# A Mamba-2 scan followed by a SiLU layer: one more pair of units multiplied in seven products, with the plain second product of the first two units moved between

## The chip, the cores and the metric

The kernel runs on one NeuronCore of one Trainium2 chip. TensorE (PE in the profile) multiplies and writes to PSUM. VectorE (DVE), ScalarE (ACT) and GpSimd (POOL) work beside it, and SyncE (SP) issues most of the DMAs. Each engine takes its own instructions in program order, and waits on semaphores that the others raise. The metric is the device time of one execution in microseconds (us), and the number compared is the median of several runs. Before the change it is 359.44 us, the median of 3 runs from 358.6 to 359.83 us.

## The reference, cut to what matters

A state-space scan over 4 batches, 8 heads and 768 positions (head size 32, state size 16) gives a 3072 x 256 matrix, and a two-matrix layer with SiLU follows:

```
cum = cumsum(log(clip(a, 1e-6, 1)));  L = exp(cum_i - cum_j), causal, by chunk
y   = ((C B^T) * L) x  +  (C state) * exp(cum)          # then state is carried on
x   = y as (batch * seq, heads * head_dim)              # 3072 x 256
h   = x @ w_in                                          # 256 -> 2048
g   = h / (1 + exp(-h))                                 # SiLU
out = g @ w_out                                         # 2048 -> 256
```

The weights arrive as 64-bit floats. The kernel loads them as pairs of 32-bit words and rebuilds fp32 values on the chip.

## The kernel before, in words

The 3072 rows are cut into 12 units of 256 positions, three to a batch. A unit first goes through the scan, in pieces named after their functions: P (prefix product of the decays, lines 278 and 284), E (the decay triangle: clip at 315 and scan at 297), T and T2 (B and C transposed, `ce` at 359), B (`BT`, line 334) and C (`cw`, line 365), D and G (small products in PSUM tile `gy`, lines 383 and 398), S (states, line 424), M (mask times product, line 409), Y (the unit's output in PSUM, lines 452 and 461) and X (its copy to `XM`, line 470). Then comes the **first product** with `w_in`, SiLU, and the **second product** with `w_out`.

Either product can be done in two ways.

- *Plain.* `f_s1(g, j)` (line 481) does the first product of one unit: in each of eight steps j, two blocks of 128 columns with two products each, and one SiLU over both. `s2_list` (line 495) does the plain second product of units one after the other: 64 products of 128 x 128 by 256 for two units, summed in one PSUM bank (`o_ps`, a pool of one buffer), with two copies by ScalarE (line 500) and four stores when a unit is done.
- *In seven.* Two units are taken together as the two columns of a 2 x 2 block matrix, and multiplied with seven block products where the plain way takes eight (Winograd's form of Strassen's scheme). For that, sums and differences are made beforehand. Those of the weights are `SW` (first product, line 627) and `SO` (second product, line 526), made once. Those of the data are `XT` (first product, line 638) and `TN` with changes in place of `gT` (second product, `f_TS`, line 540), made for each pair.

`f_x1(G, j, ...)` is a step of the first product in seven for pair G. It uses three PSUM tiles, X, W and Y. The seven products are named W, 1, 5, 6, 7, 4 and 3, and a string in `ORDER`, one for each j, gives their order; each "s" in it is one product of a second product, drawn from the queue `S2` by `f_s2(1)`, to fill TensorE. Products 1, 6, 7 and 4 all go to X: 6 adds to what 1 left there, and must wait until ScalarE has copied X (`p1`); 7 adds again after the next copy (`u2`); 4 adds after VectorE has read X for an add (line 658). Product 5 and product 3 go to Y, and W has its own tile. Between these, a list of scan pieces for the next pair is worked off on VectorE and ScalarE (`scan_plan` and `other`).

Before the change, units 0 to 3 use the plain first product, and units 4 to 11 go in pairs G = 2 to 5. The second product is plain for units 0 and 1 and in seven for all later pairs. The order by hand at the end of the kernel is this:

1. a start in which the inputs come in, the first two scans run, weight pieces are rebuilt (`w_size` on ScalarE, `w_bits` on VectorE at lines 174 to 178 and GpSimd at line 182), and `busy(n)` gives TensorE products of zeros;
2. `steps`: the first product of units 0 and 1, mixed with weight pieces and the scan of unit 2;
3. eight steps of `f_s1(2, j)`, each with a piece of unit 3's scan and four plain second products;
4. eight steps of `f_s1(3, j)`, each with pieces of the scans of units 4 and 5 and four plain second products; `SO`, `XT` and the first sums of pair 1 are made here too;
5. pairs G = 2 to 5 with `f_x1`, filled with the second product of the pair before, and at the end the second product of pair 5.

Every engine's queue is in program order, so a piece that waits holds up all that stands behind it on its engine. `f_P01` (lines 270 and 273) makes the prefix products of units 0 and 1 together, in the start.

Of the kernel before, what the change touches and what calls it, by code (L numbers as in the profile page):

```python
# [21 lines left out]
def kernel(  # L22
# [22 lines left out]
    nc = tc.nc  # L45
# [169 lines left out]
    idle = early[:, 4].bitcast(BF16)  # L215
    nc.vector.memset(idle, 0.0)

    def busy(n, early=True):
        t = ps_o.tile([128, 512], FP32, name="o_ps") if early else ps_s.tile([128, 4, 512], FP32, name="gy")[:, 0]
        for i in range(n):  # L220
            nc.tensor.matmul(out=t, lhsT=idle[:, 0:128], rhs=idle, start=True, stop=True)

    nc.vector.memset(ach[0:A0], 0.0)

# [12 lines left out]
                                fill=1.0, base=-64 * c, channel_multiplier=1)  # L237
    tiny = const.tile([128, 1], FP32, name="tiny")
    nc.scalar.activation(tiny, idle[:, 0:1], AF.Silu)
    busy(5)  # L240
    f_A()
    ident = const.tile([128, 128], FP32, name="ident")
    nc.vector.memset(ident, 0.0)
# [23 lines left out]

    def f_P01():

        nc.vector.tensor_scalar(out=pz01.rearrange("p (c t) -> p c t", c=8)[:, :, 1:],  # L270
                                in0=pa01.rearrange("p (c t) -> p c t", c=8), scalar1=1.0, scalar2=1e-6,
                                op0=ALU.min, op1=ALU.max)
        nc.vector.tensor_tensor_scan(out=pfx01, data0=pz01, data1=one01, initial=0.0, op0=ALU.mult, op1=ALU.add)  # L273
        for u in range(2):
            PFX[u] = pfx01.rearrange("p (c t) -> p c t", c=8)[:, 4 * u:4 * u + 4]
# [212 lines left out]
    def s2_list(units):  # L488
        for g in units:
            b, t0 = at(g)  # L490
            r = out[b * S + t0:b * S + t0 + UT].rearrange("(k c i) m -> k i c m", k=2, c=2)
            o = ps_o.tile([128, 2, d_model], FP32, name="o_ps")
            for c in range(2):
                for f in range(NF):
                    nc.tensor.matmul(out=o[:, c], lhsT=GTS[g][:, f, 128 * c:128 * c + 128], rhs=w_out_sb[:, f, :],  # L495
                                     start=(f == 0), stop=(f == NF - 1), skip_group_check=True)
                    if f == NF - 1 and c == 1:
                        for e in range(2):
                            o_sb = ppool.tile([128, UT], FP32, name="ps")
                            nc.scalar.activation(o_sb, o[:, e], AF.Copy)  # L500
                            for k in range(2):
                                nc.sync.dma_start(out=r[k][:, e], in_=o_sb[64 * k:64 * k + 64])
                    yield
# [108 lines left out]


    wj = w_in_sb.rearrange("p k (j i f) -> p k i j f", i=2, f=128)
    SW, XT = [], []

    def spare(d, n):
        t = rawp.tile([128, 2, WF, 2], U32, name="raw").bitcast(FP32)
        return t.rearrange("p k f two -> p (k f two)").rearrange("p (a b) -> p a b", b=n) if d is None else t

    def f_SW(i):

        t = spare(None, 128)
        SW.append(t)
        a0, a1, op = ((wj[:, 0, 1], wj[:, 1, 1], ALU.add), (SW[0], wj[:, 0, 0], ALU.subtract),
                      (wj[:, 0, 0], wj[:, 0, 1], ALU.subtract), (wj[:, 1, 0], SW[min(i, 1)], ALU.subtract))[i]
        nc.gpsimd.tensor_tensor(out=t, in0=a0, in1=a1, op=op)

    def xm2(u):
        return XM[u].rearrange("p (w c) t -> p w (c t)", w=2)  # L630

    def f_XT(G, i):

        if len(XT) < 2 and i == 0:
            XT.append(spare(None, UT))
        t, b0, b1 = XT[G % 2], xm2(2 * G), xm2(2 * G + 1)
        a0, a1 = ((b1[:, 0], b0[:, 0]), (b1[:, 1], t[:, 0]), (b1[:, 1], b1[:, 0]), (b0[:, 1], t[:, 1]))[i]
        nc.gpsimd.tensor_tensor(out=t[:, i], in0=a0, in1=a1, op=ALU.subtract)
# [2 lines left out]

    ORDER = ("W15s6sss7sss43", "W1s56ss7sss43s", "W1ss56ss7ss43s", "W1sss56ss7ss43",
             "W1ss6ss57sss43", "W1sss6ss57ss43", "W1s56sss7ss43s", "W1s56sss7sss43")

    def f_x1(G, j, dve, act):
        u0, u1 = 2 * G, 2 * G + 1
        if j == 0:
            for u in (u0, u1):
                GTS[u] = gpool.tile([128, NF, UT], FP32, name="gT")
        g0, g1, t = GTS[u0], GTS[u1], XT[G % 2]  # L650
        b0, b1 = xm2(u0), xm2(u1)
        X, W, Y = (ps_h.tile([128, 512], FP32, name="hp")[:, 0:UT] for _ in range(3))

        def mm(o, w, x_, start=True):
            nc.tensor.matmul(out=o, lhsT=w, rhs=x_, start=start, stop=True, skip_group_check=True)  # L655

        def add(o, p, q):
            nc.vector.tensor_tensor(out=o, in0=p, in1=q, op=ALU.add)  # L658

        def silu(o, i):  # L660
            nc.scalar.activation(o, i, AF.Silu)  # L661

        def other(todo, n):
            for _ in range(min(n, len(todo))):
                todo.pop(0)()

        def copy(name, i):
            o = sc.tile([128, UT], FP32, name=name)
            nc.scalar.activation(o, i, AF.Copy)  # L669
            return o  # L670

        done, first = "", 3 if j in (1, 4) else 2
        for what in ORDER[j]:
            done += what
            if what == "s":
                f_s2(1)
            elif what == "W":
                mm(W, wj[:, 1, 0, j], b0[:, 1])
            elif what == "1":
                mm(X, wj[:, 0, 0, j], b0[:, 0])  # L680
                p1 = copy("p1", X)
                add(g0[:, 2 * j], W, p1)
                other(dve, 2 if j in (2, 5) else 0)
            elif what == "5":
                mm(Y, SW[0][:, j], t[:, 0])
                p5 = copy("p5", Y)
            elif what == "6":
                mm(X, SW[1][:, j], t[:, 1], False)
                u2 = copy("u2", X)
                silu(g0[:, 2 * j], g0[:, 2 * j])  # L690
                other(dve, first)
            elif what == "7":
                mm(X, SW[2][:, j], t[:, 2], False)
                add(g1[:, 2 * j + 1], X, p5)
                silu(g1[:, 2 * j + 1], g1[:, 2 * j + 1])
            elif what == "4":
                mm(X, wj[:, 1, 1, j], t[:, 3], False)
                silu(g0[:, 2 * j + 1], X)
                other(dve, 2)
            elif what == "3":  # L700
                mm(Y, SW[3][:, j], b1[:, 1], False)
                add(g1[:, 2 * j], Y, u2)
                silu(g1[:, 2 * j], g1[:, 2 * j])
            if what in "56" and "5" in done and "6" in done:
                other(act, 9)
        other(dve, 9)
        assert not dve and not act
        if j == 7:
            XM.pop(u0)
            XM.pop(u1)  # L710
# [33 lines left out]
    def scan_plan(G):  # L744
        plan = [([], [], []) for _ in range(8)]
        for i in range(2):
            u, j = 2 * G + i, 3 * i
            E0 = [partial(f_E0, u, q, 2) for q in range(2)]
            E1 = [partial(f_E1, u, q, 4) for q in range(4)]
            plan[j][0].extend([partial(f_P0, u), partial(f_P1, u), E0[0], E0[1], E1[0], E1[1]])  # L750
            plan[j][1].extend([partial(f_T2, u, 0), partial(f_T2, u, 1)])
            plan[j + 1][0].extend([E1[2], E1[3], partial(f_B, u), partial(f_C, u)])
            plan[j + 1][2].append(partial(f_G, u))
            plan[j + 2][0].extend([partial(f_S, u, 0, 2), partial(f_S, u, 2, 4), partial(f_M, u, 0),
                                   partial(f_M, u, 1)])
# [12 lines left out]
    f_Ab(0, 0)  # L768
    f_Ab(0, 1)
    f_G0(0)  # L770
    busy(4)
    f_Ek(0, 0)
    f_Ek(0, 1)
    f_B(0)
# [8 lines left out]
    w_bits(0, 2)  # L783
    f_Ab(1, 0)
    w_size(1)
    busy(4)
    f_Y(0)
    f_Ab(1, 1)
    f_X(0)
# [36 lines left out]
            else:  # L826
                scan_piece(2, 0, step)

    for g, j, todo in steps:
        f_s1(g, j)  # L830
        w_steps(todo)
    load_unit(3)
    late = ("b13 s14", "b14 s15", "b15")
    S2.append(s2_list((0, 1)))
    for j in range(8):
        f_s1(2, j)
        scan_piece(3, j, ("", "", "T", "E", "BS", "G", "S", "Y"))
        f_s2(4)
        if j < len(late):
            w_steps(late[j])  # L840
        if j in (2, 5):
            load_unit(4 + j // 3)

    def sums(P, qs):

# [1 line left out]
            f_TS(P, 0, q, nc.gpsimd)  # L847
            f_TS(P, 2, q, nc.gpsimd)

    for j in range(8):  # L850
        f_s1(3, j)
        scan_piece(4, j, ("TE", "BS", "G", "Y", "", "", "", ""))
        scan_piece(5, j, ("", "", "T", "E", "BS", "G", "Y", ""))
        scan_piece(6, j, ("",) * 7 + ("t",))
        f_s2(4)
        if j in (2, 5):
            load_unit(6 + j // 3)
        if j in (1, 4, 6, 7):
            f_SO(len(SO))
        if j == 7:  # L860
            for i in range(4):
                f_XT(2, i)
        if j == 5:
            sums(1, (0, 1))
    for G in range(2, NU // 2):
        S2.append(s2_pair(G - 1))
        more = G + 1 < NU // 2
        plan = scan_plan(G + 1) if more else [([], [], []) for _ in range(8)]
        for j, (dve, act, pe) in enumerate(plan):
# [4 lines left out]
            for what in waiting:  # L874
                what()

            if j == 1:
                sums(G - 1, (2, 3) if G == 2 else (3,))
            if j == 1 or j == 4:
                for q in range(4):  # L880
                    f_TS(G - 1, (1, 3)[j // 4], q, nc.gpsimd)
            if j == 6 and more:
                for i in range(4):
                    f_XT(G + 1, i)
# [45 lines left out]
```

## Time and profile before

| what | value |
|---|---|
| median of 3 runs | 359.44 us |
| span of the profiled execution | 356.3 us |
| TensorE busy | 344.3 us (97%), 3276 records |
| VectorE busy | 183.2 us (51%) |
| ScalarE busy | 160.7 us (45%) |
| GpSimd busy | 181.9 us (51%) |
| share of PE in the chain that ended last | 91% |
| mean granted TensorE clock | 0.996 |
| DMA, mean over the span | 74 GB/s |

A line of the timeline gives start and length in us, the engine, the line of the kernel, the operation, tiles written and read, shape, how many instructions were merged, and in brackets the idle time before and what ended it. An fp32 product of 128 x 128 by 256 appears as two TensorE records. A record's busy time overlaps that of the next one, so the spacing of starts, and not the mean length, is what a product takes out of TensorE's time. Slices of busy time say which engine is full in which stage: an average over the whole span hides that VectorE is 93% busy from 27.65 to 55.31 us (25.75 of 27.66 us), and 46% busy from 116.97 to 170.82 us.

### The profile page before, as it was taken

To read this page: it belongs to the slowest core of one execution; us is meant where nothing else is said; L and a number is where in the kernel's file an instruction comes from. 1 tells how busy PE (TensorE), PEld (TensorE's weight loads), DVE (VectorE), ACT (ScalarE), POOL (GpSimd) and SP (SyncE) were. 2 spreads that over 40 slices of the span, in tenths; PEclk is the share of its full clock that TensorE was granted. 3 is DMA by queue.
4 is the path that set the end of the run, shared out by engine and by line. 5 is a ranking of instruction groups with operands and counts; after the bars stand their busy time and mean duration, and the time that the engine had idled before them with its cause. 6 is when DMAs were issued, how large, how long until landed. Compare 5 with 4: busy or idle time off the path is not lost.

```text
span 356.3 us, 8309 instructions
## 1 busy us (share of the span) xinstructions
PE 344.3 (97%) x3276; PEld 289.0 (81%) x3277; DVE 183.2 (51%) x389; ACT 160.7 (45%) x390; POOL 181.9 (51%) x246
## 2 busy tenths in 40 slices
PE   7879999999999999999999999999999999999994
PEld 2457888888888888888888888888888888888883
DVE  7978999554447444643454633455632221214722
ACT  2649575223222545545544545544545454453100
POOL 4434345524059076498274398264398930596100
PEclk9999999999999999999999999999999999999998
DMA  6898966871455270161026253110001010001203
GB/s 118 211 338 139 328 192 113 139 115 50 99 109 76 63 110 7 46 110 29 15 53 108 44 99 42 16 18 2 15 2 18 15 17 0 15 2 20 40 2 45
DMA packets 110059, 26.53 MB, mean 74 GB/s; under 512 B 98884, under 2 KB 105796, under 8 KB 110020
## 3 DMA queue, kind: packets, MB, share of 16 engines
q1 hardware_dynamic: 107044, 25.67, 35.5%
q10 hardware_dynamic: 2976, 0.33, 0.6%
q8 instruction: 26, 0.43, 0.5%
q14 instruction: 13, 0.11, 0.1%
HBM read 22.83 MB, written 3.15 MB: 73 GB/s over the span
## 4 chain that ended last, share of the span: by engine, by line
PE 91%; DVE 4%; DMA 2%; issue 1%; POOL 0%; SPq 0%; ACT 0%; ACTq 0%; DVEq 0%
PE o_ps L572 30%; PE hp L655 28%; PE hp L481 15%; PE o_ps L495 8%; PE hp L572 3%; PE gy L461 3%; PE gy L452 2%; PE gy L398 2%; DVE E L297 1%; PE gy L383 1%; DVE wv L178 1%; DMA tbc<-in_C_dram 1%; DMA tbc<-in_B_dram 1%; DMA out_dram<-ot 0%; DVE gT L273 0%
## 5 line engine op out<-in xcount | busy, mean ns | idle before, releaser
L658 DVE TENSOR_TENSOR gT<-hp,p 128x256 f32<-128x256 f32 x64 | 26.9, 420 | 84.6 <-ACT p L669 47.5
L481 PE MATMUL hp<-XM,w_in_sb 128*128 128x256 f32 x256 | 59.4, 381 | 1.9 <-POOL w_in_sb L182 1.1
L661 ACT ACTIVATE gT<-gT 128x256 f32<-128x256 f32 x96 | 39.7, 413 | 42.8 <-DVE gT L658 42.8
L334 POOL TENSOR_TENSOR BT<-bn,E 128x256 f32<-128x256 f32 x12 | 9.0, 751 | 94.5 <-PE hp L655 29.6
L572 PE MATMUL o_ps<-gT,w_out_sb 128*128 128x256 f32 x224 | 56.5, 379 | 0.0
L481 PEld LDWEIGHTS hp<-XM,w_in_sb 128*128 128x128 f32 x256 | 48.0, 190 | 9.7 <-POOL w_in_sb L182 2.4
L655 PE MATMUL hp<-raw 128*128 128x256 f32 x192 | 52.7, 380 | 0.0
L540 POOL TENSOR_TENSOR gT<-gT 128x256 f32<-128x256 f32 x72 | 51.3, 745 | 0.0
L572 PEld LDWEIGHTS o_ps<-gT,w_out_sb 128*128 128x128 f32 x224 | 42.4, 190 | 5.9
L655 PEld LDWEIGHTS hp<-raw 128*128 128x128 f32 x192 | 36.2, 190 | 5.4 <-POOL ps L543 0.6
L483 ACT ACTIVATE gT<-hp 128x512 f32<-128x512 f32 x32 | 19.1, 596 | 40.1 <-PE hp L481 40.1
L669 ACT ACTIVATE p<-hp 128x256 f32<-128x256 f32 x64 | 24.6, 384 | 27.5 <-PE hp L655 25.7
L658 DVE TENSOR_TENSOR gT<-hp,u 128x256 f32<-128x256 f32 x32 | 13.6, 424 | 40.8 <-PE hp L655 40.8
L655 PE MATMUL hp<-XM,w_in_sb 128*128 128x256 f32 x128 | 34.1, 389 | 0.0
L543 POOL TENSOR_TENSOR ps<-ps 128x256 f32<-128x256 f32 x28 | 20.4, 729 | 26.0 <-ACT ps L579 12.7
L495 PE MATMUL o_ps<-w_out_sb,gT 128*128 128x256 f32 x128 | 30.9, 384 | 0.0
L540 POOL TENSOR_TENSOR TN<-gT 128x256 f32<-128x256 f32 x40 | 28.8, 745 | 0.0
L495 PEld LDWEIGHTS o_ps<-w_out_sb,gT 128*128 128x128 f32 x128 | 23.8, 190 | 3.8 <-issue 0.5
L655 PEld LDWEIGHTS hp<-XM,w_in_sb 128*128 128x128 f32 x128 | 23.3, 190 | 4.3 <-issue 1.0
L297 DVE TENSOR_TENSOR_SCAN E<-ab,diag 128x256 f32<-128x256 f32 (+1 forms) x32 | 24.5, 804 | 3.7 <-PE gy L461 3.4
L540 POOL TENSOR_TENSOR gT<-gT,TN 128x256 f32<-128x256 f32 x32 | 22.2, 743 | 0.0
L579 ACT ACTIVATE ps<-o_ps 128x256 f32<-128x256 f32 x31 | 11.9, 384 | 18.5 <-PE o_ps L572 18.1
(121 smaller groups left out, 543.0 us busy)
## 6 DMA issues: line engine op xcount, KB each, us to landing
ab<-in_a_dram SPq DMA_DIRECT2D x40, 128.0 KB, 3.7
raw<-in_moe_w_in_dram SPq DMA_DIRECT2D x8, 512.0 KB, 8.1
raw<-in_moe_w_out_dram SPq DMA_DIRECT2D x8, 512.0 KB, 6.5
xt<-in_x_dram SPq DMA_DIRECT2D x24, 128.0 KB, 4.1
out_dram<-ot SPq DMA_DIRECT2D x76, 32.0 KB, 1.7
bn<-in_B_dram SPq DMA_DIRECT2D x22, 64.0 KB, 5.1
tbc<-in_C_dram SPq DMA_DIRECT2D x40, 32.0 KB, 2.1
pa<-in_a_dram SPq DMA_DIRECT2D x10, 128.0 KB
```

What stands on the lines that cost most here:

```text
L297: nc.vector.tensor_tensor_scan(out=E[u].rearrange("p k h t -> p (k h t)")[:, Q * g0:Q * (g0 + n)], data0=t.rearrange("p g t -> p (g t)"), ...
L481: nc.tensor.matmul(out=hp[:, i], lhsT=w_in_sb[:, kc, f * 128:(f + 1) * 128], rhs=xm[:, kc], start=(kc == 0), stop=(kc == KC - 1))
L483: nc.scalar.activation(GTS[g][:, 2 * j:2 * j + 2], hp, AF.Silu)
L495: nc.tensor.matmul(out=o[:, c], lhsT=GTS[g][:, f, 128 * c:128 * c + 128], rhs=w_out_sb[:, f, :], start=(f == 0), stop=(f == NF - 1), skip_ ...
L540: engine.tensor_tensor(out=o[:, j], in0=a0[:, j], in1=a1[:, j], op=ALU.subtract)
L543: engine.tensor_tensor(out=o, in0=p, in1=q, op=ALU.add)
L572: nc.tensor.matmul(out=o, lhsT=w(j), rhs=g()[:, j], start=(j == 0), stop=(j == NF // 2 - 1))
L579: nc.scalar.activation(pn, on, AF.Copy)
L655: nc.tensor.matmul(out=o, lhsT=w, rhs=x_, start=start, stop=True, skip_group_check=True)
L658: nc.vector.tensor_tensor(out=o, in0=p, in1=q, op=ALU.add)
L661: nc.scalar.activation(o, i, AF.Silu)
L669: nc.scalar.activation(o, i, AF.Copy)
```

## The change

Units 2 and 3 (pair G = 1) also go through `f_x1`. For this, unit 3's scan and `SW` must be complete before the pair begins, so a gap opens in the first products between units 0 and 1 and the pair. It is filled with 40 of the 64 plain second products of units 0 and 1; the other 24 go between the products of the pair, by new strings `ORDER1`. The loop over pairs starts at 1 in place of 2. Around it:

- `SW` is made on VectorE in place of GpSimd;
- the clip in `f_P01` (line 270) is made on GpSimd in place of VectorE;
- `s2_list` runs over f outside and over the two column blocks inside, so that its first products need only the first weight pieces;
- the loads of units 3, 4 and 5 are issued at other points, and the sums of pair 1 and the pieces of `SO` move into the steps of G = 1;
- one piece of the E scan of units 4 and 5 moves one step ahead;
- the products of zeros become 64 x 64 x 64 in place of 128 x 128 x 512, and 40, 24 and 32 in place of 5, 4 and 4.

```diff
     def busy(n):
-            nc.tensor.matmul(out=t, lhsT=idle[:, 0:128], rhs=idle, start=True, stop=True)
+            nc.tensor.matmul(out=t[:64, :64], lhsT=idle[:, 0:64], rhs=idle[:, 64:128], start=True, stop=True)
...
-    busy(5)
+    busy(40)
...
-        nc.vector.tensor_scalar(out=pz01.rearrange("p (c t) -> p c t", c=8)[:, :, 1:],
+        nc.gpsimd.tensor_scalar(out=pz01.rearrange("p (c t) -> p c t", c=8)[:, :, 1:],
...
-            for c in range(2):
-                for f in range(NF):
+            for f in range(NF):
+                for c in range(2):
...
-        nc.gpsimd.tensor_tensor(out=t, in0=a0, in1=a1, op=op)
+        nc.vector.tensor_tensor(out=t, in0=a0, in1=a1, op=op)
...
+    ORDER1 = ("W1ss56s7s43",) + ("W15s6s7s43",) * 7
...
-        for what in ORDER[j]:
+        for what in (ORDER1 if G == 1 else ORDER)[j]:
...
+            n = 3 if G == 2 else 2
+            plan[j][0].extend([partial(f_P0, u), partial(f_P1, u), E0[0], E0[1]] + E1[:n])
...
-    busy(4)
+    busy(24)
...
-    busy(4)
+    busy(32)
...
-    for j in range(8):
-        f_s1(2, j)
-        scan_piece(3, j, ("", "", "T", "E", "BS", "G", "S", "Y"))
-        f_s2(4)
...
+    for n, what in ((8, "b13 s14"), (6, "b14 s15"), (6, "T b15"), (6, "E D C"), (6, "S G"), (8, "S S S Y")):
+        f_s2(n)
...
+    load_unit(5)
+    for i in range(4):
+        f_XT(1, i)
+    for i in range(2):
+        f_T(4, i)
...
-    for j in range(8):
-        f_s1(3, j)
-        scan_piece(4, j, ("TE", "BS", "G", "Y", "", "", "", ""))
-        scan_piece(5, j, ("", "", "T", "E", "BS", "G", "Y", ""))
-        f_s2(4)
...
-    for G in range(2, NU // 2):
-        S2.append(s2_pair(G - 1))
+    for G in range(1, NU // 2):
+        if G > 1:
+            S2.append(s2_pair(G - 1))
...
+            if j in (1, 5, 6, 7) and G == 1:
+                f_SO(len(SO))
```

More of the change, by code (lines that the diff above doesn't have):

```diff
@@ L216, with busy @@
     nc.vector.memset(idle, 0.0)
-    def busy(n, early=True):
-        t = ps_o.tile([128, 512], FP32, name="o_ps") if early else ps_s.tile([128, 4, 512], FP32, name="gy")[:, 0]
+    def busy(n):
+        t = ps_o.tile([128, 512], FP32, name="o_ps")
         for i in range(n):
-            nc.tensor.matmul(out=t, lhsT=idle[:, 0:128], rhs=idle, start=True, stop=True)
+            nc.tensor.matmul(out=t[:64, :64], lhsT=idle[:, 0:64], rhs=idle[:, 64:128], start=True, stop=True)
     nc.vector.memset(ach[0:A0], 0.0)
@@ L492, in s2_list @@
             o = ps_o.tile([128, 2, d_model], FP32, name="o_ps")
-            for c in range(2):
-                for f in range(NF):
+            for f in range(NF):
+                for c in range(2):
                     nc.tensor.matmul(out=o[:, c], lhsT=GTS[g][:, f, 128 * c:128 * c + 128], rhs=w_out_sb[:, f, :],
-                                     start=(f == 0), stop=(f == NF - 1), skip_group_check=True)
+                                     start=(f == 0 and c == 0), stop=(f == NF - 1), skip_group_check=True)
                     if f == NF - 1 and c == 1:
@@ L614 @@
     wj = w_in_sb.rearrange("p k (j i f) -> p k i j f", i=2, f=128)
-    SW, XT = [], []
+    SW, XT = [], {}
     def spare(d, n):
@@ L632, in f_XT @@
     def f_XT(G, i):
-        if len(XT) < 2 and i == 0:
-            XT.append(spare(None, UT))
+        if G % 2 not in XT:
+            XT[G % 2] = spare(None, UT)
         t, b0, b1 = XT[G % 2], xm2(2 * G), xm2(2 * G + 1)
@@ L749, in scan_plan @@
             E1 = [partial(f_E1, u, q, 4) for q in range(4)]
-            plan[j][0].extend([partial(f_P0, u), partial(f_P1, u), E0[0], E0[1], E1[0], E1[1]])
+            n = 3 if G == 2 else 2
+            plan[j][0].extend([partial(f_P0, u), partial(f_P1, u), E0[0], E0[1]] + E1[:n])
             plan[j][1].extend([partial(f_T2, u, 0), partial(f_T2, u, 1)])
-            plan[j + 1][0].extend([E1[2], E1[3], partial(f_B, u), partial(f_C, u)])
+            plan[j + 1][0].extend(E1[n:] + [partial(f_B, u), partial(f_C, u)])
             plan[j + 1][2].append(partial(f_G, u))
@@ L827, in w_steps @@
                 scan_piece(2, 0, step)
-    for g, j, todo in steps:
+    for n, (g, j, todo) in enumerate(steps):
         f_s1(g, j)
         w_steps(todo)
-    load_unit(3)
-    late = ("b13 s14", "b14 s15", "b15")
+        if n == 7:
+            load_unit(3)
+    load_unit(4)
     S2.append(s2_list((0, 1)))
-    for j in range(8):
-        f_s1(2, j)
-        scan_piece(3, j, ("", "", "T", "E", "BS", "G", "S", "Y"))
-        f_s2(4)
[L839 to L842, printed above, removed]
+    for n, what in ((8, "b13 s14"), (6, "b14 s15"), (6, "T b15"), (6, "E D C"), (6, "S G"), (8, "S S S Y")):
+        f_s2(n)
+        for step in what.split():
+            if step[0] in "sb":
+                w_steps(step)
+            else:
+                scan_piece(3, 0, step)
+    load_unit(5)
[3 more added lines that the diff above has]
+        f_T(4, i)
     def sums(P, qs):
@@ L848, in sums @@
             f_TS(P, 2, q, nc.gpsimd)
-    for j in range(8):
-        f_s1(3, j)
-        scan_piece(4, j, ("TE", "BS", "G", "Y", "", "", "", ""))
-        scan_piece(5, j, ("", "", "T", "E", "BS", "G", "Y", ""))
-        scan_piece(6, j, ("",) * 7 + ("t",))
-        f_s2(4)
[L856 to L864, printed above, removed]
-    for G in range(2, NU // 2):
-        S2.append(s2_pair(G - 1))
+    for G in range(1, NU // 2):
+        if G > 1:
+            S2.append(s2_pair(G - 1))
         more = G + 1 < NU // 2
@@ L875 @@
                 what()
-            if j == 1:
-                sums(G - 1, (2, 3) if G == 2 else (3,))
-            if j == 1 or j == 4:
+            if j in (1, 4) and G > 1:
+                if j == 1:
+                    sums(G - 1, (3,))
                 for q in range(4):
                     f_TS(G - 1, (1, 3)[j // 4], q, nc.gpsimd)
+            if j in (1, 5, 6, 7) and G == 1:
+                f_SO(len(SO))
             if j == 6 and more:
```

## The prediction

> **What bounds the kernel now.** I read four views. Page part 1 puts TensorE at 97% of the span, the others near half. Its list of waits says where it stands still: eight waits, the longest 1.5 us, all before 27.65 us. So I cut the time there and took busy time by stage:
>
> ```profile
> 0.00:27.65 27.65, 20.50 (x361) 11.87 (x362) 21.73 (x45) 12.44 (x25) 11.15 (x23) 1.00 0.87 226
> 27.65:55.31 27.66, 27.66 (x269) 23.73 (x270) 25.75 (x40) 20.87 (x39) 11.68 (x9) 1.00 0.83 212
> 55.31:116.97 61.66, 61.66 (x714) 52.30 (x712) 36.20 (x60) 18.75 (x38) 29.40 (x26) 1.00 0.55 97
> 116.97:170.82 53.85, 53.85 (x537) 45.95 (x536) 24.83 (x61) 27.42 (x74) 34.46 (x51) 1.00 0.34 60
> ```
>
> The columns are length, then busy time of PE, its weight loads, DVE, ACT and POOL. From 27.65 us PE is busy in every stage for its whole length: there, time is the number of products, plus any wait a change brings in. Before 27.65 us the chain of waits runs over DVE. The third stage is the one rewritten (plain products of units 2 and 3, second product of units 0 and 1); the fourth already runs in seven products.
>
> The timeline shows one step of the fourth stage (j = 0, fillers between). Products 6, 7 and 4 are the PE rows at 118.70, 120.42 and 122.15; ACT and DVE must read X between them:
>
> ```profile
> 118.70 0.59 PE L655 MATMUL hp<-raw 128*128 128x256 f32 x2
> 119.13 1.46 PE L572 MATMUL o_ps<-gT,w_out_sb 128*128 128x256 f32 x6
> 119.33 0.39 ACT L669 ACTIVATE u<-hp 128x256 f32<-128x256 f32 x1 [0.48 <-PE hp L655]
> 120.42 0.59 PE L655 MATMUL hp<-raw 128*128 128x256 f32 x2
> 120.85 1.46 PE L572 MATMUL o_ps<-gT,w_out_sb 128*128 128x256 f32 x6
> 121.06 0.42 DVE L658 TENSOR_TENSOR gT<-hp,p 128x256 f32<-128x256 f32 x1 [1.25 <-PE hp L655]
> 122.15 0.59 PE L655 MATMUL hp<-raw,w_in_sb 128*128 128x256 f32 x2
> ```
>
> A product is two records, 0.432 us start to start (119.13 to 120.42 is three). From 6 to the end of the copy of X is 1.02 us, from 7 to the end of the add 1.06 us; three fillers plus the product itself are 1.73 us, so nothing waits.
>
> **What the Trainium skill says.** *TensorE: Matmul & The Clock Gate*, "Back-to-back issue gap": about N/2.4 + 2.5 ns a matmul when warm; for two passes of 256 columns that is 216 ns, which is the trace's record. *Perfetto Trace Analysis*, "Tensor Engine Instruction": an instruction leaves the wait queue when its semaphores are met, and the end of a matmul is estimated. The trace agrees that 0.6 us is near the truth: ACT starts 0.63 us after product 6. *SBUF — State Buffer*, "SBUF: two separate sides": GpSimd and a VectorE operation with two SBUF inputs block one another. The trace agrees: the scan at line 284 takes 0.70 us alone, 1.66 beside GpSimd.
>
> **The change, part by part.**
>
> *Fewer products.* Two plain units take 2 x 8 x 4 = 64 products, a pair in seven takes 8 x 7 = 56. Eight fewer at 0.432: **-3.45 us**. The second product keeps its 64, so 40 go into the gap and 24 between the products of the pair.
>
> *The gap* (PE from 55.31). 32 fillers end at 69.1, D and G of unit 3 (1.1) at 70.2, 8 fillers at 73.7, Y (1.4) at 75.1. Beside it: VectorE finishes E of unit 3 at 67.75 as before (its order up to there is unchanged), SW piece 0 next, S and M after G, about 72.1, ahead of Y; SW pieces 1 to 3 at some 1.2 us each (twice line 526's quiet 0.67, less overhead) end at 75.7, transposes of unit 4 at 76.8. Weight piece 15 is ready at 64.0 (line 182's last end), its first filler comes at 55.31 + 28 x 0.432 = 67.4. The copy out of unit 0 (two of 0.38) hides behind D and G. Loads keep their order; only unit 0's store moves ahead of load 5. All hidden. Exposed: XM (0.6) at 75.8, then four differences on GpSimd at 0.72 to 1.05. Product 5 at 76.8 just finds the first, 6 and 7 miss theirs by 0.1 to 0.3. **+0.5** (0.2 to 1.2).
>
> *The pair, G = 1.* ORDER1 is W 1 5 s 6 s 7 s 4 3: one filler where the old ORDER strings have two or three. 7 is due 2 x 0.432 = 0.86 us after 6, but X is free at 1.02 + 0.05 = 1.07 (the 0.05 is what PE takes after ACT at 27.60/27.65): wait 0.21. 4 is due 0.86 after 7 and free at 1.11: wait 0.25. PE is in order, so everything queues behind, and nothing later gives it back. 8 steps x 0.46 = 3.7. In steps 2 and 5 more stands ahead of that add on VectorE:
>
> ```profile
> 131.74 0.42 DVE L658 TENSOR_TENSOR gT<-hp,p 128x256 f32<-128x256 f32 x1 [2.42 <-ACT p L669]
> 132.08 0.21 DVE L422 COPY st<-gy 128x64 f32<-128x64 f32 x1
> 132.33 0.91 DVE L424 SCALAR_TENSOR_TENSOR st<-st,pfx,gy 128x64 f32<-128x64 f32 x3
> 133.16 1.28 DVE L409 TENSOR_TENSOR E<-gy,E 128x512 f32<-128x512 f32 x2
> 134.36 0.41 DVE L658 TENSOR_TENSOR gT<-hp,p 128x256 f32<-128x256 f32 x1
> ```
>
> W of that step starts at 130.16, so the add ends 4.61 us later. Product 4 comes at 135.01 now (4.85), in the new order at 8 x 0.432 + 0.1 + 0.2 = 3.76: wait 0.9, 0.65 more than above, twice: 1.3. Step 7 has no filler left before 4 (64 = 40 + 4 + 6 x 3 + 2): 0.4 more. Sum 5.4. A restart costs extra: eight records take 1.99 us after a wait, 1.89 without, so up to 0.1 on 16 waits; I take half, 0.8 (both ends kept). **+6.2** (5.4 to 7.0). VectorE's total, some 32 us in 45, is not the limit. SO falls in steps without S and M or behind them; the third E1 piece in step 0 (0.63) stands behind that step's last add, with 2 us to the next. The new loop order of the plain second product changes neither its count nor its two copies at the end: nothing.
>
> *The start.* Line 270 moves to GpSimd, queued behind BT:
>
> ```profile
> 8.33 0.43 DVE L270 TENSOR_SCALAR gT<-gT 128x512 f32<-128x512 f32 x1
> 8.41 0.84 POOL L334 TENSOR_TENSOR BT<-bn,E 128x256 f32<-128x256 f32 x1 [3.17 <-DVE E L297]
> 8.79 1.56 DVE L273 TENSOR_TENSOR_SCAN gT<-gT 128x520 f32<-128x520 f32 x1
> 26.56 0.34 PE L461 MATMUL gy<-E,xt 64*32 64x64 f32 x15 [1.51 <-issue]
> ```
>
> The scan (line 273) then starts at 9.25 plus line 270 on GpSimd. *GPSIMD Engine Reference*, "Elementwise": 512 elements at 1.8 cycles are 0.77 us, an estimate for a one-input operation; this trace has 0.67 (an affine select of that shape) and 1.31 (two inputs) around it. So 10.1, not 8.79. The scan, no longer beside GpSimd, should take about 1.2 (line 297's 512 columns, 1.19) instead of 1.56: end 11.3 against 10.35, +0.9 (0.5 to 1.5), and VectorE's queue behind it leads to 27.65.
>
> The zeros: 5 products of 512 columns took 2.1 us; 40 small ones with their loads take 0.05 to 0.11 each (the clock-gate page's cold N/1.2, with and without a load of 64 columns beside it), 2.1 to 4.3. The first real products then start at 3.4 to 5.6, and E wants the first one (1.7 cold) at 6.05: 0 to 1.2 late, I take 0.2. The other two groups lie in idle time. Against this stands the 1.51 us "issue" wait. Queue q8 brought instructions in 26 parts; if they are PE's (6,553 records), a part holds some 250, and 166 more ahead (83 products, 83 loads) move that boundary to near 20 us, where the DMA is full too but VectorE has other work: -0.5 (-1.5 to 0). Together **+0.6** (-1.0 to +2.7).
>
> Sum: -3.45 + 0.5 + 6.2 + 0.6 = +3.85, so **363.3 us**.
>
> **Rivals.** *A, the waits don't show*: reads of X are released sooner than the rows' ends, or the longer gaps in front absorb them. Only steps 2 and 5 would pay about 1 us: -3.45 + 0.3 + 1 - 0.3 = -2.4, **357.0, faster**. For it: PE's ends are modelled, and the start may gain. Against: DVE at 121.06 did wait for PE, so the 1.06 us are real. *B, VectorE is late into the pair*: SW at GpSimd's 2.35 a piece rather than 1.2, as when blocked, moves its queue by 3.5 us and the first 4 by about 3: **366.3**. Against: GpSimd is idle when pieces 1 to 3 run. *C, half the waits*: +3.1 in place of 6.2, about **360.2**.
>
> **Chances.** Forecast 0.58, A 0.18, B 0.12, C 0.12. A falls nearly all under 358.4, C half within 0.3%. Faster 0.18, same 0.09, slower 0.73. The forecast's bounds run from 360.6 to 366; I leave out most of A and the far end of B: 359.4 to 366.5.
>
> **What would show it.** Right: PE waits at line 657 on ACT and on DVE, 0.2 to 0.3 us each, two in every step, near 0.9 in steps 2 and 5; PE no longer busy throughout between 75 and 122 us; SW ending before 77. Wrong: that stage at PE's full busy time (A falls out), or a first step with a wait over 1 us (B). For the start: whether the gap-free run begins before or after 27.65. If it moves by over 2 us, the start decides and my sum is wrong.

## The result, and the profile after

The changed kernel takes **364.93 us** (median of 4 runs, 363.29 to 365.4), where the kernel before takes 359.44: a ratio of 1.0148, with a 95% interval from 1.0111 to 1.0184. It is 5.5 us slower. The forecast was 363.3 us, with a range of 359.4 to 366.5.

The profiled execution has a span of 363.1 us against 356.3. That is 6.8 us, more than the 5.5 of the medians, because the profiled execution of the kernel before took 358.11 us, 1.3 below its median. First the busy time by stage of the changed kernel; the columns are length, then busy time of PE, its weight loads, DVE, ACT and POOL (with counts), granted TensorE clock, DMA share and GB/s. The stages are the first 32 plain second products; the waiting for D and G of unit 3; the last 8 second products; and, after unit 3's Y, the new pair G = 1.

```profile
52.68:66.60 13.92, 13.92 (x65) 11.97 (x63) 13.56 (x20) 5.05 (x9) 5.80 (x5) 1.00 0.69 122
66.60:70.14 3.54, 1.53 (x65) 1.06 (x65) 1.51 (x2) 0.66 (x2) 2.04 (x2) 0.84 1.20 150
70.14:74.91 4.77, 4.77 (x25) 3.76 (x17) 4.49 (x9) 0.64 (x2) 0.00 (x0) 0.76 0.58 124
76.20:123.61 47.41, 44.69 (x479) 32.51 (x473) 29.45 (x66) 25.64 (x68) 17.85 (x24) 1.00 0.48 80
```

Before the change PE was busy for the full length of these stages. Now three lines differ from that. In the second, PE stands still for 2.0 of 3.54 us. In the third it is busy throughout, but at a clock of 0.76. In the fourth, 2.7 us are idle, and more is lost inside the records: the stage holds 80 products at 0.432 us (34.6 us) and D, G and Y of two units (4.8 us), so 39.4 us of work, and it lasts 47.4.

The list of waits of PE in the changed kernel (total us, times, longest) names the first two places; the eight waits of the kernel before had none of them:

```profile
PE gy L383 <- POOL BT L334: 2.0, 1, 2.0
PE hp L657 <- DVE gT L660: 2.0, 4, 0.7
```

The two short waits of every step are too short for this list. One step of the pair shows them, in the timeline of PE (start, length, line, operation, tiles). Line 657 is a product of the first product in seven (line 655 before), line 495 a filler:

```profile
83.75 0.59 PE L657 MATMUL hp<-raw 128*128 128x256 f32 x2
84.18 0.59 PE L495 MATMUL o_ps<-w_out_sb,gT 128*128 128x256 f32 x2
84.82 0.70 PE L657 MATMUL hp<-raw 128*128 128x256 f32 x2
85.36 0.59 PE L495 MATMUL o_ps<-w_out_sb,gT 128*128 128x256 f32 x2
86.03 0.70 PE L657 MATMUL hp<-raw,w_in_sb 128*128 128x256 f32 x2
86.57 0.59 PE L657 MATMUL hp<-XM,raw 128*128 128x256 f32 x2
```

These are 6, filler, 7, filler, 4, 3. Read the spacing of starts: without a wait it is 0.43. From the filler at 84.18 to product 7 it is 0.64 (0.21 late, for ScalarE's copy), and from the filler at 85.36 to product 4 it is 0.67 (0.24 late, for VectorE's add). Behind each of the two, the next product comes after 0.54 instead of 0.43. That makes 0.67 us in a step whose waits no list shows.

Where the 6.8 us between the two profiled spans lie, in the trace: the run without gaps in the first products begins 0.75 earlier (26.90 for 27.65); eight fewer products give 3.45; the wait for `BT` costs 2.0; the low clock 1.6 (G takes 1.16 where it takes 0.69 at full clock, the 8 fillers 4.83 where they take 3.72); the pair loses 8.0. The sum is 7.4. That is 0.6 more than the spans differ, and I can't assign this 0.6; it is what is left between sums of many short records.

### The profile page after: what moved, and what is told of

The parts are those of the page before. It is cut to its first block, busy times and chain, and to the rows that moved or that the text cites. A ratio compares the mean times of both kernels' runs of the same rounds, so it can differ in the third digit from the quotient of the medians.

```text
span 363.1 us, 8526 instructions
## 1 busy us (share of the span) xinstructions
PE 348.3 (96%) x3344; PEld 288.3 (79%) x3344; DVE 196.5 (54%) x424; ACT 171.9 (47%) x430; POOL 175.4 (48%) x247
## 4 chain that ended last, share of the span: by engine, by line
PE 83%; SPq 4%; DVE 4%; DMA 3%; issue 3%; POOL 1%; ACT 1%; ACTq 0%; DVEq 0%; POOLq 0%
PE hp L657 34%; PE o_ps L572 29%; PE hp L481 6%; PE hp L572 3%; PE o_ps L495 3%; PE gy L461 2%; SPq L107 2%; PE gy L398 2%; PE gy L452 2%; DMA tbc<-in_B_dram 1%; DVE gT L660 1%; PE gy L383 1%; DMA tbc<-in_C_dram 1%; SPq L156 1%; SPq L122 1%
## 5 line engine op out<-in xcount | busy, mean ns | idle before, releaser
L660 DVE TENSOR_TENSOR gT<-hp,p 128x256 f32<-128x256 f32 x80 | 33.6, 420 | 89.7 <-ACT p L671 49.5
L663 ACT ACTIVATE gT<-gT 128x256 f32<-128x256 f32 x120 | 49.6, 414 | 52.3 <-DVE gT L660 52.2
L657 PE MATMUL hp<-raw 128*128 128x256 f32 x240 | 67.9, 384 | 0.4
L657 PEld LDWEIGHTS hp<-raw 128*128 128x128 f32 x240 | 44.3, 190 | 10.4 <-ACT u L671 3.1
L671 ACT ACTIVATE p<-hp 128x256 f32<-128x256 f32 x80 | 30.7, 383 | 34.5 <-PE hp L657 31.9
L657 PE MATMUL hp<-XM,w_in_sb 128*128 128x256 f32 x160 | 42.8, 390 | 0.0
L657 PEld LDWEIGHTS hp<-XM,w_in_sb 128*128 128x128 f32 x160 | 29.0, 189 | 5.5 <-issue 1.4
L543 POOL TENSOR_TENSOR ps<-ps 128x256 f32<-128x256 f32 x28 | 20.3, 728 | 26.1 <-ACT ps L579 12.8
L481 PE MATMUL hp<-XM,w_in_sb 128*128 128x256 f32 x128 | 29.3, 383 | 1.3 <-ACT XM L470 0.7
L481 PEld LDWEIGHTS hp<-XM,w_in_sb 128*128 128x128 f32 x128 | 23.7, 190 | 5.8 <-POOL w_in_sb L182 1.7
L657 PE MATMUL hp<-raw,w_in_sb 128*128 128x256 f32 x80 | 24.6, 389 | 2.3 <-DVE gT L660 2.0
L657 PE MATMUL hp<-XM,raw 128*128 128x256 f32 x80 | 23.8, 379 | 0.0
L663 ACT ACTIVATE gT<-hp 128x256 f32<-128x256 f32 x40 | 15.3, 383 | 17.1 <-PE hp L657 16.8
```

The source lines that it names most:

```text
L481: nc.tensor.matmul(out=hp[:, i], lhsT=w_in_sb[:, kc, f * 128:(f + 1) * 128], rhs=xm[:, kc], start=(kc == 0), stop=(kc == KC - 1))
L543: engine.tensor_tensor(out=o, in0=p, in1=q, op=ALU.add)
```

## The experiments

Each is compared with the kernel before on the same chip, where that took 359.48, 359.25 or 359.73 us; a difference between two medians from different chips can be off by some tenths. Two theories stood at first. **X's chain**: PE waits for the readers of PSUM tile X in every step, and this is what costs the time. **The gap**: the stage in which fillers cover the scan of unit 3 doesn't close, and costs it.

### The readers of X taken away

```diff
-                u2 = copy("u2", X)
+                u2 = copy("u2", p1 if G == 1 else X)
...
-                add(g1[:, 2 * j + 1], X, p5)
+                add(g1[:, 2 * j + 1], W if G == 1 else X, p5)
```

A first form (free_x) let the add read Y in place of W:

> The changed kernel, except that in pair G = 1 the second copy by ScalarE reads the first copy (in SBUF) in place of X, and the add before product 4 reads Y in place of X: products 7 and 4 have nothing to wait for. Left out by this: the right values of two of the four SiLU inputs of units 2 and 3; the amount of work on each engine is the same. Theory (the waits of 7 and 4 on X are what the pair costs): the pair, 47.4 us in the profile after against 39.4 us of products, loses some 7 us of its 8; the total falls from 364.9 to 357 to 358.5, below the kernel before. Rival (the pair is slow because VectorE, the weight loads or the clock cannot follow at one filler to a gap): the pair stays above 44 us and the total above 362.

It took 360.25 us (358.55 to 362.11), a ratio of 1.0011 [0.9991, 1.0031]. The pair fell from 47.41 to 43.20 us, less than expected, and the reason is a wait of my own making: product 3 writes Y, and now had to wait for the add that reads it. In steps 2, 5 and 7 this wait stands in the timeline of PE:

```profile
90.51 0.70 PE L657 MATMUL hp<-XM,raw 128*128 128x256 f32 x2 [0.58 <-DVE gT L660]
```

So the wait was moved, not taken away. The second form (free_x2) reads W, which nothing writes again within the step:

> As free_x, but the add before product 4 reads W in place of Y, so that product 3 has no new wait either (free_x left 3.8 us of waits in the pair, of which 1.9 stand before product 3 in steps 2, 5 and 7). Left out again: right values of two SiLU inputs of units 2 and 3. Theory (waits on what a later product overwrites are all that the pair loses): the pair takes 40.5 to 41.5 us in place of 43.2 with free_x and 47.4 after, total 357.5 to 358.8, below the kernel before. Rival (VectorE's queue in steps 2, 5 and 7 holds the pair up by itself): the pair stays near 43 us and the total near 360.

It took **358.89 us** (357.3 to 361.55), 0.9987 [0.9957, 1.0018]. The pair took 41.23 us, as expected; the total is 0.1 us above the range given. Its step on PE, from the filler behind 6 to product 3:

```profile
84.53 0.59 PE L495 MATMUL o_ps<-w_out_sb,gT 128*128 128x256 f32 x2
84.96 0.59 PE L657 MATMUL hp<-raw 128*128 128x256 f32 x2
85.39 0.59 PE L495 MATMUL o_ps<-w_out_sb,gT 128*128 128x256 f32 x2
85.82 0.59 PE L657 MATMUL hp<-raw,w_in_sb 128*128 128x256 f32 x2
86.25 0.59 PE L657 MATMUL hp<-XM,raw 128*128 128x256 f32 x2
```

Every spacing is 0.43, and the 0.70 of a product that had waited is 0.59. The waits on X are worth 47.41 - 41.23 = 6.2 us in the pair and 364.93 - 358.89 = 6.0 us in the median. With them, the change loses 5.5; without them, it is level with the kernel before. But this kernel still has the new start, and the kernel before with that start alone takes 358.17 us (start_only, below; a ratio of 0.9974 for 0.9987). So even without the waits on X, nothing of the 3.45 us saved is seen: the gap (3.6 us) and what else the pair loses (41.23 - 39.4 = 1.8 us) use it up.

### Fillers put elsewhere

If the waits are for want of fillers between 6, 7 and 4, the same fillers in a better order must give part of it back. A step has ten products in the mean (seven and three fillers), 4.32 us. X alone needs 1 to 6, 6 to 7, 7 to 4 and 4 to the next 1: two of these links take 1.07 and 1.21 us in the changed kernel's step above (83.75 to 84.82 to 86.03, the second with 0.1 for the restart behind a wait), and the other two go through ScalarE like the first. Four of about 1.07 are 4.3 us (an estimate from these rows), so no order leaves room to spare. The strings (spread) put more fillers where VectorE is late, and move product 5 or 3 in between where its inputs allow it:

```diff
-    ORDER1 = ("W1ss56s7s43",) + ("W15s6s7s43",) * 7
+    ORDER1 = ("sW1s563s7ss4", "W1s657s34", "W1sss65s73s4", "W156s73s4s",
+              "W1s65734", "W1ss65ss7s34", "W156s73s4", "W15637s4")
```

> The changed kernel with other strings ORDER1 only: the same 7 products and in all the same 24 fillers, but product 3 ahead of 4, 5 between 6 and 7, and more fillers in steps 2 and 5. Theory (each of the gaps 1-6, 6-7, 7-4 on X needs 1.07 to 1.11 us, and a gap of 0.86 us costs 0.2 to 0.25 plus a 0.1 restart): by the same working, step by step, the pair takes 44.3 us in place of 47.4, total 361.5 to 362.5. Rival (waits on X do not set the pair's time): no change, 364.9 within 0.5.

362.30 us (360.65 to 363.88), 1.0094 [1.0063, 1.0125]; the pair took 44.77 us. Both as expected: 2.6 of the 6.2 us come back by this order alone, and the rest doesn't.

### The gap kept warm

The wait for `BT` is 2.0 us long, and after it the granted clock is half for a while: 0.50 from 71 to 72 us in the changed kernel. Zero products ahead of D show what the clock alone is worth:

```diff
         f_s2(n)
+        if what == "S G":
+            busy(36)
```

> The changed kernel with 36 more small products of zeros between the 32nd filler and the product D of unit 3, where TensorE stands still for 2.0 us. Theory (that stillness lowers the granted clock to a half for the next 3 us, and G and the 8 fillers behind it then take 0.5 and 1.2 us more than their usual time): with the zeros the clock stays at 1.0, G takes 0.69 and the 8 fillers 3.6 us, Y starts 1 to 1.7 us earlier, total 363.2 to 364. Rival (G and the fillers are slow for another reason, DMA traffic or PSUM): they stay slow and the total stays at 364.9 or rises a little.

364.29 us (363.2 to 365.7), 1.0139 [1.0105, 1.0173]. In the timeline of PE the zeros, and then the eight fillers at their full speed:

```profile
69.80 1.30 PE L221 MATMUL o_ps<-gT 128*64 128x64 bf16 x36 [0.75 <-ACT ps L500]
...
72.09 3.72 PE L495 MATMUL o_ps<-w_out_sb,gT 128*128 128x256 f32 x16
```

From the first filler to Y the stage took 20.68 us where the changed kernel took 22.23, the expected 1.55 less. The median fell by only 0.6, just less than expected, and its interval overlaps that of the changed kernel. In this execution the start was 2.4 us later (29.30 for 26.90), because the low clock fell there: after two waits of 1.76 and 0.89 us it was 0.50 from 15 to 21 us, and eight records of line 481 took 3.62 us where they take 1.9 at full clock. And not every execution has the low clock in the gap to begin with (free_x has the same wait of 2.01 us, and then 3.72 for the eight fillers). The low clock is shown where it falls; what it costs in the median is not settled.

### The start, part by part

Three kernels change only the start of the kernel before. zeros_only has the small products of zeros, p01_only has line 270 on GpSimd, start_only has both.

```diff
-            nc.tensor.matmul(out=t, lhsT=idle[:, 0:128], rhs=idle, start=True, stop=True)
+            nc.tensor.matmul(out=t[:64, :64], lhsT=idle[:, 0:64], rhs=idle[:, 64:128], start=True, stop=True)
...
-    busy(5)
+    busy(40)
...
-        nc.vector.tensor_scalar(out=pz01.rearrange("p (c t) -> p c t", c=8)[:, :, 1:],
+        nc.gpsimd.tensor_scalar(out=pz01.rearrange("p (c t) -> p c t", c=8)[:, :, 1:],
...
-    busy(4)
+    busy(24)
...
-    busy(4)
+    busy(32)
```

> The kernel before with only the two changes of the start: the products of zeros small and many, and line 270 on GpSimd. Theory (more instructions ahead move the fetch of TensorE's instructions away from the critical Y of unit 1, saving 1.5 us, and the scan at line 273 starts 1.2 us later, of which 0.8 are left): the run without gaps begins at 26.9 in place of 27.65, total 358.7 within 0.5, that is 0 to 1 us below before. Rival (the earlier begin in the profile after was chance of one execution): 27.65 or later, total 359.4 or above.

> The kernel before with the small and many products of zeros alone, line 270 still on VectorE. Theory (the instruction fetch that stops TensorE at 25.05 us moves to an earlier place where it is not on the chain, and the scan at line 273 keeps its 8.79 us): no issue wait in Y of unit 1, the gap-free run begins at 26 to 26.8 us, total 357.4 to 358.4, as start_only or some 0.5 us below it. Rival (line 270 on GpSimd is what gains): 27.65 and 359.4, no change.

> The kernel before with line 270 on GpSimd alone. Theory: the scan at line 273 starts at 10.0 in place of 8.79 us, ends 0.8 us later, and VectorE's queue carries that to the begin of the gap-free run, 28.2 to 28.6 us with the issue wait still in Y of unit 1; total 359.9 to 360.5. Rival (this move is what gains): begin at 27 or below, total 358.2.

| kernel | median, us | before, same chip | ratio to before |
|---|---|---|---|
| start_only | 358.17 (357.6 to 359.56) | 359.48 | 0.9974 [0.9949, 0.9999] |
| zeros_only | **356.64** (356.47 to 358.67) | 359.25 | 0.9939 [0.9914, 0.9963] |
| p01_only | 361.29 (358.56 to 363.59) | 359.25 | 1.0059 [1.0032, 1.0087] |

The small zeros gain: by the ratios 0.6% alone (2.2 us; 2.6 by the medians on that chip), and 0.85% (3.1 us) with line 270 on GpSimd. The move of line 270 costs 0.6% alone (2.1 us). With the small zeros it costs 0.35% (1.3 us), but there the two intervals overlap. zeros_only gained more than expected, p01_only lost more, and start_only came out at the lower edge of what was expected. zeros_only is the fastest kernel of this study. In the timelines, zeros_only on the first line and p01_only below:

```profile
26.11 4.15 PE L481 MATMUL hp<-XM,w_in_sb 128*128 128x256 f32 x18 [0.69 <-ACT XM L470]
```

```profile
9.90 1.24 DVE L273 TENSOR_TENSOR_SCAN gT<-gT 128x520 f32<-128x520 f32 x1 [1.46 <-POOL gT L270]
...
27.43 0.34 PE L461 MATMUL gy<-E,xt 64*32 64x64 f32 x15 [1.59 <-issue]
28.52 1.78 PE L481 MATMUL hp<-XM,w_in_sb 128*128 128x256 f32 x7 [0.74 <-ACT XM L470]
```

The run without gaps begins at 26.11 and 28.52, against 27.65 before. With line 270 moved, the scan behind it ends at 11.14 instead of 10.35, and the run begins 0.87 later; the wait named "issue" stays. With small zeros this wait is gone from Y of unit 1, in every profile.

The profile of start_only does not fit its theory: the run begins at 27.87, not at 26.9, although the total fell. An "issue" wait of 0.68 us now stands in Y of unit 0, and behind it the granted clock is 0.50 from 16 to 19 us. The two records of line 305 take 2.08 us, where they take 1.13 in the kernel before:

```profile
15.54 0.46 PE L461 MATMUL gy<-E,xt 64*32 64x64 f32 x33 [0.68 <-issue]
15.93 2.08 PE L305 MATMUL hp<-gT 108*128 108x512 f32 x2
```

The medians move by more than the beginnings do (2.6 against 1.5; 2.0 against 0.9). The rest goes with the clock. Among the executions whose mean granted clock was 0.995 or more, the medians are 358.09 us before (28 of 58 on that chip), 356.62 with zeros_only (10 of 13) and 358.94 with p01_only (6 of 20). These lie 1.5 and 0.9 us apart, as the beginnings do; the executions below 0.995 take 1.9 to 2.9 us more. So the start also changes how often an execution gets the lower clock. That this comes from the length of its waits is not shown.

### Line 270 moved back

If the move costs 1.5 to 1.9 us, as the medians taken without regard to the chip say, undoing it in the changed kernel must show it (after_v):

```diff
-        nc.gpsimd.tensor_scalar(out=pz01.rearrange("p (c t) -> p c t", c=8)[:, :, 1:],
+        nc.vector.tensor_scalar(out=pz01.rearrange("p (c t) -> p c t", c=8)[:, :, 1:],
```

> The changed kernel with line 270 back on VectorE; nothing else differs. If the move of line 270 costs by itself what it cost alone (361.29 against 359.44, and 358.17 against 356.64 with the small zeros in both: some 1.5 to 1.9 us), this kernel takes 363.0 to 363.6, the scan of line 273 ends near 10.4 rather than 11.3, and the gap-free run begins near 26.1. Rival: the start is held by the instruction-fetch wait or the clock, not by that scan; then the time stays within 0.5 us of 364.9.

363.87 us (362.69 to 366.1), 1.0112 [1.0066, 1.0159]. The median is 1.1 lower than the changed kernel's, less than expected, and the intervals overlap. In its profile the scan is early as expected (it ends at 10.5), but an "issue" wait of 1.83 us ends at 15.88 us, the granted clock behind it is 0.50 from 16 to 19 us, and the run begins at 28.12 instead of 26.1. So in this execution, the slowest of the four, the start was held as the rival has it. All four comparisons of this move (with the one below) point the same way; its size in the changed kernel stays open.

### All three mendings together

all3 is the changed kernel with the spread strings, 12 zero products ahead of D, and the first piece of `SW` put behind unit 3's mask, so that it no longer runs beside `BT`:

```diff
-    for n, what in ((8, "b13 s14"), (6, "b14 s15"), (6, "T b15"), (6, "E D C"), (6, "S G"), (8, "S S S Y")):
+    for n, what in ((8, "b13 s14"), (6, "b14 s15"), (6, "T b15"), (6, "E D C"), (6, "G"), (8, "S S S S Y")):
         f_s2(n)
+        if what == "G":
+            busy(12)
```

> The changed kernel with the strings of spread, SW piece 0 after the mask of unit 3 in VectorE's queue (so that BT on GpSimd isn't slowed, 0.64 in place of 1.39 us, and D comes 0.7 us earlier), and 12 small products of zeros before D. Theory: 2.6 from the strings, 0.7 from D, and the 1.6 us of lower clock where it occurs: total 359.5 to 361. Rival (the gap and the pair are limited together by VectorE's chain, and what D gains the pair loses): no better than spread, 362.

361.18 us (360.68 to 363.84), 1.0056 [1.0034, 1.0077], just above the range. D starts at 67.82 in place of 68.66, the low clock is gone, and the pair begins at 73.78 in place of 76.20. But 1.2 us are given back in the pair's first step (75.61 to 77.24 is 1.63 for one product), where `XT` isn't ready yet:

```profile
77.24 0.70 PE L658 MATMUL hp<-raw 128*128 128x256 f32 x2 [0.98 <-POOL raw L638]
```

By the trace, most of this wait is made by the mending itself. The last piece of `SW`, now later on VectorE, and the second of GpSimd's differences `XT` run side by side and take 1.76 and 1.60 us, where they take 1.22 and 0.74 in the changed kernel: the same trouble as between `SW` and `BT`, moved. With line 270 moved back as well (all3_v):

> The kernel with spread fillers, the first SW piece behind the mask and 12 zero products ahead of D, with line 270 back on VectorE. If that move costs 1.5 to 1.9 us whatever stands behind it, this takes 359.3 to 359.8, level with the kernel before. Rival as in the other run: no gain, near 361.2.

360.81 us (360.45 to 363.69), 1.0048 [1.0024, 1.0072]: 0.4 lower, not told apart from all3. With these mendings the change still costs 0.5%. Against zeros_only, which has the same start without the change, it costs 1.1% (ratios of 1.0048 and 0.9939).

## Why the prediction was right or wrong, point by point

**Direction and main cause: right, and shown.** The step "two waits in every step of G = 1" is what makes the kernel slower. It was put at +6.2 us, and taking X's readers away gives 6.2 us in the pair. The waits of 0.21 and 0.25 read 0.21 and 0.24. That the two sums are equal is in part luck: by the spacings, the waits and restarts come to 7.0, and free_x2 has a new wait of 0.46 at the end of its pair (117.53 to 118.42 is 0.89), where the next product waits for VectorE's add. Rivals A (no waits) and C (half of them) fall: the pair's PE is not busy throughout, and the sum is whole.

**The pair's sum: the waits right, the restart too small, one term missing.** All losses in the pair are 8.0, not 6.2; by the trace, the eight steps lose 1.08, 0.75, 1.47, 0.76, 0.75, 1.15, 0.76 and 1.32. The waits on X among them are 5.5 (5.4 put), though not all where they were put: step 5 has 0.75 (1.1 put), step 7 has 1.2 (0.9 put) and step 0 has 0.6 (0.46 put). The restart was taken at half of 0.1; it is 0.1 in full (0.54 for 0.43), some 1.5 in place of 0.8. The last 1.0 was put nowhere in the pair: about 0.1 at each change between the products and D, G or Y (93.37 to 93.89 is 0.52), and 0.23 in step 0, where `XT` is late as the term of the gap had expected. In step 7 `SO` stands on VectorE from 119.01 to 120.98 ahead of an add, which I had put "behind" such adds. Step 2 went as predicted. VectorE does S, then the mask, then the add for which product 4 waits:

```profile
90.03 1.22 DVE L424 SCALAR_TENSOR_TENSOR st<-st,pfx,gy 128x64 f32<-128x64 f32 x4
91.16 1.28 DVE L409 TENSOR_TENSOR E<-gy,E 128x512 f32<-128x512 f32 x2
92.36 0.42 DVE L660 TENSOR_TENSOR gT<-hp,p 128x256 f32<-128x256 f32 x1
92.83 0.70 PE L657 MATMUL hp<-raw,w_in_sb 128*128 128x256 f32 x2 [0.70 <-DVE gT L660]
```

**The gap: wrong.** Put at +0.5, it cost 3.6: 2.0 of waiting, 1.6 of low clock. The step that failed is "PE from 55.31". I took 55.31 for the end of the first products of units 0 and 1, but that merged record held eight records of `f_s1(2, 0)` as well. Counted from the start of the run, those products take 25.78 us (26.90 to 52.68 in the changed kernel), so they end at 53.43 in the time of the prediction, not 55.31. So there was 1.9 us less work ahead of the fillers. With the start 0.75 earlier as well, they ended at 66.65 and not at 69.1, ahead of the end of E of unit 3 (67.0), and D had to wait for what I had called hidden. A second miss lengthened the wait. `SW` on VectorE and `BT` on GpSimd came to run side by side:

```profile
66.92 1.20 DVE L627 TENSOR_TENSOR raw<-w_in_sb 128x1024 f32<-128x1024 f32 x1
67.22 1.39 POOL L334 TENSOR_TENSOR BT<-bn,E 128x256 f32<-128x256 f32 x1 [3.96 <-PE o_ps L495]
68.66 0.46 PE L383 MATMUL gy<-xt,BT 64*32 64x64 f32 x32 [2.01 <-POOL BT L334]
```

`BT` takes 0.64 alone (at 85.53 in this trace) and 1.39 here. This is the case of the Trainium skill's page *SBUF — State Buffer*, "SBUF: two separate sides", that the prediction named for another pair of lines, and did not apply to this one; all3, with `SW` behind, has `BT` at 0.64 and D 0.84 us earlier (0.1 of it from an earlier start). That the clock would fall after a 2 us wait was not considered at all.

**VectorE late into the pair (rival B): falls.** `SW` took 1.2 us a piece, as worked out, and ended at 76.0. The first step's wait at product 4 was 0.35 (80.31 to 81.09 is 0.78 for 0.43), not over 1.

**The start: wrong in sign.** Put at +0.6, with a range from -1.0. The medians of start_only and the kernel before give -1.3 (-0.9 by the ratio), and the run in the changed kernel's profile begins 0.75 earlier. Of its terms, line 270 was close: it took 0.61 (0.77 estimated), and the scan ended at 11.26 (11.3 predicted), which p01_only carries through as 0.87. The zeros cost nothing: 40 small ones take 2.35 us, the five large ones 2.32. The term that was too small is the fetch wait, put at -0.5: in this execution it left the chain altogether. It does not always, as start_only and after_v show, and where it comes back it stands at 15 to 16 us and not near 20.

```profile
10.02 1.24 DVE L273 TENSOR_TENSOR_SCAN gT<-gT 128x520 f32<-128x520 f32 x1 [1.45 <-POOL gT L270]
26.90 14.08 PE L481 MATMUL hp<-XM,w_in_sb 128*128 128x256 f32 x64 [0.69 <-ACT XM L470]
```

That the total came within 1.6 us is in part luck, because the errors went both ways: the start 1.4 us better than put, the gap and the rest of the pair about 5 worse in the profiled execution, with 0.6 unassigned and a median difference 1.3 below that of the spans, for the reason given with the result.

## What to carry to other kernels

Saving products on a full TensorE pays only if the remaining order still covers the round trip of each PSUM tile: count the products between a write and the next write of the same tile, and compare with the round trip in your trace (about 1.1 us here, for fp32 products of 256 columns and a reader of 128 x 256), before counting what is saved. Where a stage is closed by fillers, fix its borders by counting products from a known start, not from the edge of a merged record, and look at what each other engine does in the last microsecond before the border. And measure small side changes by themselves: here the smaller products of zeros alone were worth 2.2 to 2.6 us, against 3.45 for the eight products saved, and without that comparison the change looks better than it is.

## What the runs showed of the hardware

- **A 2 us wait can halve TensorE's clock.** In the changed kernel, spread, free_x2 and after_v, a wait of 2.0 us was followed by low clock: the eight fillers took 4.83, 5.29, 5.17 and 4.97 us. In free_x, after the same wait, they took 3.72. In the start of p01_only it was 0.50 from 14 to 17 us after a wait of 1.98 us; free_x and all3 have one of 1.76 us there and keep full clock. The Trainium skill, *TensorE: Matmul & The Clock Gate*, "What's actually happening", has half speed after one idle window of some 3.4 us, windows that run free of the program. The halving agrees (0.50); here an idle time of 2.0 us was enough in four of five profiles, so the measurement differs from the page. That the place of the wait in such a window decides is argued, not tested.
- **A wait costs PE 0.1 us beyond itself**: the product behind one that waited starts 0.54 us later instead of 0.43. A change from these products to the small ones of D, G and Y costs about the same (0.52 from 93.37 to 93.89).
- **The "issue" wait sits at fixed places in PE's instructions.** By the trace's records, 345 products stand ahead of it in the kernel before and in p01_only; 221 in start_only, after_v, spread, free_x2 and warm_gap; five other profiles with small zeros have none. The distance is 124 or 125 products (one of the large zero products has no record), some 250 instructions with their weight loads. The Trainium skill, *Runtime: NRT & Kernel Launch*, "Instruction fetch mechanics", has instructions brought in by blocks of 256, at a cost mostly hidden. The spacing is near that, so these waits are taken for fetches, which no run shows directly; if they are, the cost was not hidden in this start, with 0.68 to 1.83 us. Why some executions wait at such a place and others don't stays open.
